# Key sums of the wide attention tiles from products with a constant column, in place of ScalarE's accumulator

## The chip, the cores and the metric

One core of a Trainium2 chip runs the whole program in one launch. The metric is the time of one execution on the device in microseconds (us), as the median of several runs. The profile is of one more execution of the same program.

## The reference

The program computes an attention stage and two feed-forward stages over 2304 tokens (4 batches of 576), in float32:

```python
a = softmax(scale * mean4(q) @ mean4(k)^T) @ mean4(v)      # 4 tokens averaged, every head
l = softmax(where(|i - j| < 4, scale * q @ k^T, -1e9)) @ v  # local band of 7 keys
x = repeat(a, 4) + l                                        # each softmax divides by its sum + 1e-9
xn = x / sqrt(mean(x*x) + 1e-6) * rms_g
h = (silu(xn @ w_gate) * (xn @ w_val)) @ w_out              # 512 -> 1536 -> 512
out = relu(h @ w_in)**2 @ w_out2                            # 512 -> 2048 -> 512
```

## The kernel before, in words

The feed-forward stages are float32 products, each made of three products of split operands (`xh`, `xl` are the high and low part of the activations, `whi`, `wlo` of the weights). The tokens are cut into nine blocks of 256. For block `j` and slice `fp` of the first hidden layer, `hidden` (L920) makes 24 gate products into bank `g` and 24 value products into bank `v`, and `outp` (L946) adds 24 products into banks `a` or `b`. One product of 256 columns is one instruction; there are 4080 of them, and 1632 of 512 columns in the second stage.

Before a block can be multiplied, its tokens must have gone through the attention stage. Batch 0 (blocks 0 and 1, and 64 tokens of block 2) goes through `wide` and `wide_post`: six tiles of 96 tokens (`WT`), each with a band of 104 keys (`WK`) and 8 heads. `wide(t)` (L702) makes the scores of the tile's 8 heads on TensorE, takes the maximum over the keys on VectorE, multiplies the maxima by the scale (L721), and runs one exponential per head on ScalarE (L725). Those 8 instructions per tile also give the sums over the keys through `accum_out`; L727 and L728 add 1e-9 to them and take the reciprocal, both on VectorE and in SBUF (`sums`, 96 x 8). Then the weights are transposed on TensorE and copied to `pt`. `wide_post(t)` (L737) multiplies `pt` with the values (L746, 8 products of 64 columns), spreads the averaged attention over the tokens (L751, 4 products of 128 columns), multiplies by the reciprocal of the sums, adds, squares and sums on ScalarE, takes the power on GpSimd, scales, transposes (L765) and writes `xh` and `xl` (L775, L776). The averaged attention itself comes from `down(b, pr)` (L614): per pair of heads three products of 144 columns, transposes, and 8 products of 65 columns. The other batches go through `attend` (a local attention on VectorE and GpSimd) and `post`.

The weights of the feed-forward stages are packed and are decoded on the chip: `decode` (L543) runs some seven instructions of 512 columns per half tile on ScalarE, VectorE and GpSimd. All of this preparation overlaps with the products as far as it can.

The order of the work is not the order of the source. Every operation is recorded with its dependences, and `Plan.trace` (L434) sets one order for all engines by planning: `PLAN` gives the order in which the steps are recorded (d: `down`, a: `wide`, b: `wide_post`, w: weights of a slice and kind, u: `attend`, p: `post`, x: `hidden` of one slice and `outp` of the one before), and the planner passes `ROUNDS` times over the operations, each time with first positions from the pass before, shifted at random by up to `JIT`, and keeps the best pass of its own reckoning. `TAGS` names the PSUM banks of each step, `SLOT` the buffers of the weights. On each engine instructions run in the order that comes out.

One more thing of the planner matters here. Until the first real product into the bank `v`, it fills planned idle time of TensorE with products of the identity with itself into that bank, which nobody reads:

```python
fill = fill and not op.ends
if fill and free:
    for _ in range(int((s - free) * FILL / 0.22)):
        self.nc.tensor.matmul(out=out, lhsT=one, rhs=one, start=True, stop=True)
```

They stand at L466 of the profile; all other instructions are issued by L473. `op.ends` (L333) is true of the first operation that writes bank `v` otherwise. From there on no fill product is made.

Of the kernel before, what the change touches and what calls it, by code (L numbers as in the profile page):

```python
# [17 lines left out]
AF = mybir.ActivationFunctionType  # L18
ALU = mybir.AluOpType
# [9 lines left out]
SCALE = 0.125  # L29
# [3 lines left out]
WT, WK = 96, 104  # L33
# [13 lines left out]


TAGS = ('dbg- dtg- dbg- dgg- bdd- bdd- bdd- bdd- ttd- ttd- ttd- ttd- add- add- add- add- '
        'aagg aagg aagt bbtd bbdd bbtd bdt tdt gta gdt gdt btt '  # L50
        '-- -- a3 a3 -- -- -- -- -- -- -- -- -- -- -- -- -- -- -- g1 g1 -- -- -- -- -- -- -- -- -- -- -- -- -- -- --')
SEQ = '011100001101'
PLAN = 'd2 d3 d0 d1 a0 b0 w00 a2 a1 w01 w12 b1 a4 b2 a3 a5 w11 w21 b4 w20 w10 b3 w02 w30 u1 w32 b5 d7 u0 d5 d4 d6 w22 E w31 w41 w40 w50 x x w42 x x d10 x x w52 w51 x x x x x p2 x u2 d11 u3 p3 x d8 x x u5 d9 u4 x x x p4 u6 x x d12 x x x d15 d14 d13 x u7 p5 u8 x u9 x x x x x p6 x x x u10 x x x u11 x x p7 x x u12 u13 x x x x x x x x p8 x x x x x x'
SLOT = [7, 8, 9, 1, 0, 4, 5, 2, 6, 3, 0, 1, 3, 4, 5, 2]
ROUNDS = 38
HIDE = 0.14
W2ST = 6
BEGIN = 1.6
# [1 line left out]
SPARE = {'A': 0.6, 'V': 2.2, 'P': -0.1}  # L60
SLACK = 0.02
FILL = 0.8
JIT = 0.3
SEED = 1


# [410 lines left out]
def attn_moe_kernel(ctx: ExitStack, tc, qs, kw, vw, qt, kt, vt, v4, wg, wv, wo, w2i, w2o, gw, gb,  # L477
                    msk, band, up, ones, ident, out):
    plan = Plan(tc.nc, tc, ctx)
    V, A, P, T, DQ, VP, AV = (plan.engine(e) for e in ("V", "A", "P", "T", "D", "VP", "AV"))  # L480

    start = [sum(BLK[:j]) for j in range(len(BLK) + 1)]
# [16 lines left out]
    def bank(tag, dtype=F32):  # L499
        return tile("ps", tag, [128, 512], dtype, 2 if tag in "ab" else 1)  # L500
# [8 lines left out]
    half_neg = tile("const", "half", [128, 8])  # L509
# [192 lines left out]
    def wide(t):  # L702

        v = wvs[t % len(wvs)]
        DQ.dma_start(out=v, in_=vt[WT * t:WT * t + WK])
        p, pt = wps[t % len(wps)], wpts[t % len(wpts)]
        bd = band_sb[:, 0 if t == 0 else 2 if t == S // WT - 1 else 1].unsqueeze(1).to_broadcast([WT, 4, WK])
        tags = TAGS.split()[16 + t]
        sp = [bank(tags[h])[0:WT, 0:4 * WK].rearrange("p (r k) -> p r k", r=4) for h in range(2)]
        with plan.joint():  # L710
            for h in range(2):
                T.matmul(out=sp[h], lhsT=id_sb[0:WT, 0:WT], rhs=bd, start=True, stop=False, skip_group_check=True)
            for r in range(4):
                for h in range(2):
                    hs = slice(64 * h, 64 * h + 64)
                    T.matmul(out=sp[h][:, r], lhsT=wq[r][hs, WT * t:WT * t + WT], rhs=wk[r][hs, WT * t:WT * t + WK],
                             start=False, stop=(r == 3), skip_group_check=True)
        nm, sm_ = small[t % 2][0], sums[t]
        for h in range(2):
            V.tensor_reduce(out=nm[:, 4 * h:4 * h + 4], in_=sp[h], axis=AX.X, op=ALU.max, negate=True)  # L720
        V.tensor_scalar(out=nm, in0=nm, scalar1=SCALE, scalar2=None, op0=ALU.mult)  # L721
        for h in range(2):
            for r in range(4):
                i = 4 * h + r
                A.activation(p[:, h, r], sp[h][:, r], AF.Exp, bias=nm[:, i:i + 1], scale=SCALE,  # L725
                             accum_out=sm_[:, i:i + 1])
        V.tensor_scalar(out=sm_, in0=sm_, scalar1=1e-9, scalar2=None, op0=ALU.add)  # L727
        V.reciprocal(out=sm_, in_=sm_)  # L728
        for h in range(2):
            tp = bank(tags[2 + h])[0:WK, 0:4 * WT].rearrange("p (r k) -> p r k", r=4)  # L730
            with plan.joint():
                for r in range(4):
                    T.transpose(tp[:, r], p[:, h, r], id_sb[0:WT, 0:WT])
            AV.copy(pt[:, h], tp)
        wx[t] = pt, v, sm_

    def wide_post(t):  # L737

        pt, v, rs = wx.pop(t)
        tags = TAGS.split()[22 + t]  # L740
        x = bank(tags[0])[0:WT]
        with plan.joint():
            for r in range(4):
                for h in range(2):
                    es = slice(128 * r + 64 * h, 128 * r + 64 * h + 64)
                    T.matmul(out=x[:, es], lhsT=pt[:, h, r], rhs=v[:, es], start=(r == 0 and h == 0),  # L746
                             stop=(r == 3), skip_group_check=True)
        y = bank(tags[1])[0:WT]
        with plan.joint():
            for r in range(4):  # L750
                T.matmul(out=y[:, 128 * r:128 * r + 128], lhsT=up_sb[:, t % 3], rhs=wod[r][:, t // 3],  # L751
                         start=(r == 0), stop=(r == 3), skip_group_check=True)
        xa, ss = wxas[t % 2], small[t % 2][1][:, 0:1]
        V.tensor_tensor(out=xa.rearrange("p (r h d) -> p r h d", r=4, h=2),
                        in0=x.rearrange("p (r h d) -> p r h d", r=4, h=2),
# [3 lines left out]
        V.tensor_scalar(out=ss, in0=ss, scalar1=1.0 / DM, scalar2=1e-6, op0=ALU.mult, op1=ALU.add)  # L759
        P.tensor_tensor(out=ss, in0=ss, in1=half_neg[0:WT, 0:1], op=ALU.pow)  # L760
        V.scalar_tensor_tensor(out=xa, in0=y, scalar=ss, in1=gb_sb, op0=ALU.mult, op1=ALU.mult)
        tp = bank(tags[2])[:, 0:4 * WT].rearrange("p (k n) -> p k n", k=4)
        with plan.joint():
            for k in range(4):
                T.transpose(tp[:, k], xa[:, 128 * k:128 * k + 128], id_sb[0:WT, 0:WT])  # L765
# [235 lines left out]
    s = 0  # L1001
    for c in PLAN.split():
        n = int(c[1:]) if c[1:] and c[0] != "w" else 0
# [175 lines left out]
```

## Time and profile before

| | before |
|---|---|
| median of 3 runs | 1000.95 us (1000.70 to 1002.62) |
| the profiled execution | 1000.25 us |
| its span, first to last instruction | 998.0 us |
| TensorE busy | 980.2 us, 98% of the span |
| VectorE busy | 587.6 us, 59% |
| ScalarE busy | 417.0 us, 42% |
| GpSimd busy | 442.3 us, 44% |

Times inside the profile count from the span's start. PE is TensorE, PEld its weight loads, DVE VectorE, ACT ScalarE, POOL GpSimd. Names of tiles stand without their numbers: `b` are the large buffers and also the PSUM banks of that letter, `w` the weight buffers, `st` the staging buffers of the decoding. A float32 product that is not split takes two passes, so 8 such products read as x16. PEclk is the share of TensorE's full clock that was granted.

### The profile page before, as it was taken

The numbers are of one execution on the slowest core, as the hardware profiler recorded it, in microseconds if no ns is written. First come the engines' busy times: TensorE is split into PE (matmuls) and PEld (weight loads), VectorE is DVE, ScalarE is ACT, GpSimd is POOL, SyncE is SP. The second block draws the span as 40 slices with busy tenths as digits, with TensorE's granted clock in tenths as the row PEclk, the third lists the DMA queues.
The fourth block names the chain that finished last, engine by engine and source line by source line (L and its number), as shares of the span: only waits on it lengthen the run. The fifth ranks groups of instructions, "written<-read, shape, count | busy, mean of one in ns | idle before, by whom it ended". The sixth has DMA issues, their size and how long they took to land.

```text
span 998.0 us, 17246 instructions
## 1 busy us (share of the span) xinstructions
PE 980.2 (98%) x6866; PEld 906.4 (91%) x6866; DVE 587.6 (59%) x985; ACT 417.0 (42%) x984; POOL 442.3 (44%) x298
## 2 busy tenths in 40 slices
PE   7998999999999999999999999999999999999998
PEld 7888999999999999999999998888888888888897
DVE  6999899786687857575634568963222322322232
ACT  5787665532435342323244557663222212322232
POOL 2566688867656676676733465863001000100000
PEclk9999999999999999999999999999999999999999
DMA  9954553253262523222011446334000100100010
GB/s 282 262 160 157 175 179 103 73 151 113 85 182 80 171 78 115 93 65 96 28 33 60 132 128 209 104 109 137 1 1 1 54 0 1 43 1 1 1 43 22
DMA packets 38465, 92.93 MB, mean 93 GB/s; under 512 B 4218, under 2 KB 14498, under 8 KB 38386
## 3 DMA queue, kind: packets, MB, share of 16 engines
q1 hardware_dynamic: 38386, 91.84, 29.6%
q8 instruction: 54, 0.88, 0.4%
q14 instruction: 25, 0.20, 0.1%
HBM read 80.62 MB, written 11.21 MB: 92 GB/s over the span
## 4 chain that ended last, share of the span: by engine, by line
PE 89%; DVE 5%; POOL 2%; DMA 2%; issue 1%; ACT 1%; SPq 0%; DVEq 0%; POOLq 0%; ACTq 0%
PE v L473 25%; PE g L473 24%; PE a L473 20%; PE b L473 15%; DVE b L473 2%; PE d L473 2%; DVE st L473 2%; PE t L473 2%; PE v L466 1%; DMA b<-in_qt 1%; DMA st<-in_wg 1%; POOL w L473 0%; POOL st L473 0%; POOL pr L473 0%; POOL b L473 0%
## 5 line engine op out<-in xcount | busy, mean ns | idle before, releaser
L473 PE MATMUL g<-xh,w 128*128 128x256 f32 (+1 forms) x776 | 176.8, 307 | 0.4 <-DVE th L473 0.4
L473 PE MATMUL v<-xh,w 128*128 128x256 f32 (+1 forms) x632 | 147.6, 311 | 0.5 <-DVE hl L473 0.5
L473 DVE SCALAR_TENSOR_TENSOR v<-v,th 128x512 f32<-128x512 f32 (+1 forms) x94 | 63.3, 674 | 128.6 <-ACT th L473 101.3
L473 PEld LDWEIGHTS g<-xh,w 128*128 128x128 f32 x776 | 131.1, 191 | 7.0 <-ACT xh L473 0.6
L473 ACT ACTIVATE th<-g 128x512 f32<-128x512 f32 (+1 forms) x94 | 54.5, 580 | 198.1 <-PE g L473 194.8
L473 POOL TENSOR_TENSOR pr<-v,es 128x896 f32<-128x896 f32 x54 | 99.4, 1939 | 65.7 <-DVE es L473 28.2
L473 PE MATMUL v<-xh,b 128*128 128x256 f32 (+1 forms) x552 | 123.9, 303 | 0.1
L473 POOL TENSOR_TENSOR pr<-k,q 128x896 f32<-128x896 f32 x54 | 115.4, 2158 | 9.6 <-DVE sc L473 7.2
L473 PE MATMUL g<-xl,w 128*128 128x256 f32 (+1 forms) x388 | 118.3, 305 | 0.1
L473 PEld LDWEIGHTS v<-xh,w 128*128 128x128 f32 x632 | 107.7, 191 | 7.1 <-PE g L473 0.7
L473 POOL TENSOR_TENSOR xl<-st,xh 128x1024 fp32r<-128x1024 f32 (+1 forms) x10 | 21.6, 2179 | 184.7 <-ACT xh L473 184.7
L473 PE MATMUL v<-xl,w 128*128 128x256 f32 (+1 forms) x316 | 97.9, 310 | 0.0
L473 PEld LDWEIGHTS v<-xh,b 128*128 128x128 f32 x552 | 93.0, 191 | 4.4 <-PE g L473 0.3
L473 PE MATMUL g<-xh,b 128*128 128x256 f32 (+1 forms) x408 | 94.4, 310 | 0.2 <-DVE th L473 0.2
L473 ACT CAST hh<-v 128x512 fp32r<-128x512 f32 (+1 forms) x94 | 53.5, 569 | 81.6 <-DVE v L473 71.3
L473 PE MATMUL v<-xl,b 128*128 128x256 f32 (+1 forms) x276 | 83.1, 301 | 0.0
L473 DVE SCALAR_TENSOR_TENSOR g<-g,th 128x512 f32<-128x512 f32 (+1 forms) x40 | 25.8, 645 | 95.5 <-ACT th L473 95.4
L473 DVE TENSOR_TENSOR hl<-v,hh 128x512 fp32r<-128x512 f32 (+1 forms) x94 | 62.4, 664 | 26.3 <-ACT hh L473 24.6
L473 PEld LDWEIGHTS g<-xl,w 128*128 128x128 f32 x388 | 74.1, 191 | 3.6 <-DVE xl L473 0.3
L473 POOL TENSOR_TENSOR st<-st 128x512 int32<-128x512 int32 x48 | 55.9, 1166 | 41.5 <-DVE st L473 39.4
L473 PEld LDWEIGHTS g<-xh,b 128*128 128x128 f32 x408 | 69.1, 190 | 4.2 <-issue 0.3
L473 ACT ACTIVATE st<-st 128x512 int32<-128x512 uint32 (+1 forms) x96 | 64.7, 684 | 18.7 <-DVE st L473 11.2
(207 smaller groups left out, 2336.8 us busy)
## 6 DMA issues: line engine op xcount, KB each, us to landing
k<-in_kw SPq DMA_DIRECT2D x12, 640.0 KB
v<-in_vw SPq DMA_DIRECT2D x12, 640.0 KB
st<-in_w2i SPq DMA_DIRECT2D x14, 512.0 KB
st<-in_w2o SPq DMA_DIRECT2D x14, 512.0 KB
y<-vv SPq DMA_DIRECT2D x18, 256.0 KB
out<-xh SPq DMA_DIRECT2D x18, 256.0 KB
st<-y SPq DMA_DIRECT2D x8, 512.0 KB
st<-in_wg SPq DMA_DIRECT2D x7, 512.0 KB
```

The source lines that it names most:

```text
L466: self.nc.tensor.matmul(out=out, lhsT=one, rhs=one, start=True, stop=True)
L473: getattr(self.hw[on[op]], method)(*args, **kw)
```

## The change

The sums over the keys no longer come from the exponentials. `wide` runs its 48 exponentials without `accum_out`. `wide_post` gets 8 products of one column per tile: the transposed weights `pt` (104 keys x 96 tokens) times a constant column of -0.5, into columns 384 to 391 of the bank that the transposes of the same tile use later. VectorE reads these sums from PSUM, multiplies by -2, adds 1e-9, and takes the reciprocal.

```diff
@@ wide
-                A.activation(p[:, h, r], sp[h][:, r], AF.Exp, bias=nm[:, i:i + 1], scale=SCALE,
-                             accum_out=sm_[:, i:i + 1])
-        V.tensor_scalar(out=sm_, in0=sm_, scalar1=1e-9, scalar2=None, op0=ALU.add)
-        V.reciprocal(out=sm_, in_=sm_)
+                A.activation(p[:, h, r], sp[h][:, r], AF.Exp, bias=nm[:, i:i + 1], scale=SCALE)
@@ wide_post, behind the products with the values
+        tp = bank(tags[2])
+        sm_ = tp[0:WT, 384:392]
+        with plan.joint():
+            for h in range(2):
+                for r in range(4):
+                    i = 4 * h + r
+                    T.matmul(out=sm_[:, i:i + 1], lhsT=pt[:, h, r], rhs=half_neg[0:WK, 0:1], start=(i == 0), stop=(i == 7),
+                             skip_group_check=True)
+        V.tensor_scalar(out=rs, in0=sm_, scalar1=-2.0, scalar2=1e-9, op0=ALU.mult, op1=ALU.add)
+        V.reciprocal(out=rs, in_=rs)
...
-        tp = bank(tags[2])[:, 0:4 * WT].rearrange("p (k n) -> p k n", k=4)
+        tp = tp[:, 0:4 * WT].rearrange("p (k n) -> p k n", k=4)
@@ numbers of the planner
-        'aagg aagg aagt bbtd bbdd bbtd bdt tdt gta gdt gdt btt '
+        'aagg aagg aagt bbtd bbdd bbtd bdt bdt gta gda gdt bdt '
...
-SLOT = [7, 8, 9, 1, 0, 4, 5, 2, 6, 3, 0, 1, 3, 4, 5, 2]
-ROUNDS = 38
+SLOT = [7, 8, 4, 1, 0, 9, 5, 2, 6, 3, 4, 1, 3, 2, 5, 0]
+ROUNDS = 14
...
-JIT = 0.3
+JIT = 0.05
```

`PLAN` is the same up to and with its first two steps x; behind them w42, w52, w51, d10, d8, u7, d13, u10, u12 and u13 stand one to some steps earlier or later among the steps x. With these numbers the planner gives another order from its start on. Two places matter below.

On TensorE, the first real product into bank `v` (`v<-xh`). Before, it stands behind 151 fill products, and behind all products with the values (96x64) of batch 0 and all but one of its groups of transposes to `xh` (128x96):

```order
L473 MATMUL b<-b_412,b_200 96x64 x8
L466 MATMUL v<-id 128x128 x19
L473 MATMUL t<-id,b_470 128x96 x4
L473 MATMUL d<-id,pe 72x96 x3
L466 MATMUL v<-id 128x128 x3
L473 MATMUL b<-b_351,qbd 96x144 x3
L473 MATMUL d<-id,pe 72x96 x3
L473 MATMUL t<-b_355,b_351 96x128
L473 MATMUL t<-b_410,b_351 96x128
L473 MATMUL t<-b_200,b_351 96x128
L473 MATMUL t<-b_294,b_351 96x128
L473 MATMUL v<-xh,w_796 128x256
```

In the change it stands behind 108 fill products, right behind the fifth of the six groups of sums (96x1):

```order
L466 MATMUL v<-id 128x128 x3
L473 MATMUL a<-half,b_358 96x1 x8
L466 MATMUL v<-id 128x128 x4
L473 MATMUL t<-id,b_502 104x96 x4
L466 MATMUL v<-id 128x128 x3
L473 MATMUL t<-half,b_402 96x1 x8
L473 MATMUL d<-id,b_502 104x96 x4
L473 MATMUL b<-b_354,qbd 96x144 x3
L473 MATMUL v<-xh,w_625 128x256
L473 MATMUL v<-xl,w_625 128x256
```

The rest of the wide tiles has moved behind the first 24 value products, between them and the first gate product, where no fill is made any more:

```order
L473 MATMUL t<-half,b_199 96x1 x8
L473 MATMUL a<-id,b_520 128x96 x4
L473 MATMUL d<-b_358,b_354 96x128
L473 MATMUL d<-b_402,b_354 96x128
L473 MATMUL d<-b_199,b_354 96x128
L473 MATMUL d<-b_298,b_354 96x128
L473 MATMUL b<-b_354,qbd 96x144 x3
L473 MATMUL g<-xh,w_450 128x256
```

On VectorE, the two instructions on the sums. Before, both work in SBUF (`b_89` to `b_89`), and the first of these rows is the scaling of the maxima, the second of that shape the addition to the sums:

```order
L473 TENSOR_SCALAR b_89<-b_89 96x8
L473 TENSOR_SCALAR st<-st 128x512
L473 TENSOR_SCALAR b_89<-b_89 96x8
L473 TENSOR_REDUCE xa<-pr 128x128
L473 TENSOR_SCALAR b_262<-b_262 128x512
L473 RECIPROCAL b_89<-b_89 96x8
```

In the change the addition reads the bank (`t`); the scaling of the maxima stays as it was:

```order
L473 TENSOR_SCALAR b_89<-b_89 96x8
L473 TENSOR_SCALAR st<-st 128x512
L473 TENSOR_SCALAR b_89<-t 96x8
L473 TENSOR_SCALAR ssum<-ssum 128x4
L473 RECIPROCAL b_89<-b_89 96x8
L473 TENSOR_SCALAR st<-st 128x512
```

## Rows read from the trace of the kernel before

**Rows 1.** The head of the page: span, busy time and share of each engine.

```profile
span 998.0 us, 17246 instructions
PE 980.2 (98%) x6866; PEld 906.4 (91%) x6866; DVE 587.6 (59%) x985; ACT 417.0 (42%) x984; POOL 442.3 (44%) x298
```

**Rows 2.** Busy time of each engine in stretches of the span.

```profile
core 0: us, PE busy (x) PEld busy (x) DVE busy (x) ACT busy (x) POOL busy (x), PEclk, DMA share, GB/s
50.00:75.00 25.00, 24.03 (x228) 21.65 (x227) 22.99 (x42) 20.74 (x61) 17.01 (x13) 1.00 0.51 160
75.00:100.00 25.00, 21.33 (x185) 20.79 (x184) 23.63 (x43) 19.13 (x47) 16.03 (x16) 0.93 0.48 156
200.00:250.00 50.00, 50.00 (x435) 50.00 (x434) 36.87 (x65) 17.23 (x50) 33.19 (x21) 1.00 0.45 132
```

**Rows 3.** PE in order of time, 30 to 106 us: start, length, instruction, wait before.

```profile
30.50 0.51 PE L473 MATMUL g<-id,b 96*104 96x96 f32 x4 [0.15 <-PE a L473]
...
79.69 1.08 PE L473 MATMUL d<-b,b 72*96 72x128 f32 x8 [1.63 <-DVE b L473]
...
95.32 0.47 PE L473 MATMUL v<-xh,w 128*128 128x256 f32 x1
...
99.47 0.90 PE L473 MATMUL b<-b,b 128*96 128x144 f32 x6
...
105.23 0.39 PE L473 MATMUL g<-xl,w 128*128 128x256 f32 x1
```

**Rows 4.** PE in order of time, products of 64 columns with the same weights as the sums.

```profile
32.75 1.50 PE L473 MATMUL b<-b,b 104*96 104x64 f32 x16
```

**Rows 5.** PE groups, 0 to 96 us: xcount | busy us, mean ns | idle before.

```profile
L466 PE MATMUL v<-id 128*128 128x128 f32 x302 | 40.9, 285 | 0.0
L473 PE MATMUL b<-w,w 64*96 64x104 f32 x48 | 2.9, 259 | 0.0
```

**Rows 6.** ACT in order of time: an exponential, its accumulator read, the next exponential.

```profile
34.06 0.33 ACT L473 ACTIVATE b<-a,b 96x104 f32<-96x104 f32 x1
34.29 0.20 ACT L473 ACTIVATION_READ_ACCUMULATOR b<-a,b 96x1 f32 x1
34.38 0.34 ACT L473 ACTIVATE b<-a,b 96x104 f32<-96x104 f32 x1
```

**Rows 7.** ACT groups, 0 to 100 us: reads of the accumulator, half of the wide tiles'.

```profile
L473 ACT ACTIVATION_READ_ACCUMULATOR b<-a,b 96x1 f32 x24 | 4.9, 203 | 0.0
```

**Rows 8.** DVE groups, 0 to 100 us: small instructions on SBUF and on PSUM.

```profile
L473 DVE TENSOR_SCALAR b<-b 96x8 f32<-96x8 f32 x12 | 5.2, 438 | 0.0
...
L473 DVE TENSOR_SCALAR b<-b 96x1 f32<-96x1 f32 x6 | 0.9, 142 | 0.0
...
L473 DVE TENSOR_SCALAR rc<-g 72x4 f32<-72x4 f32 x4 | 0.6, 150 | 1.7 <-PE g L473 1.7
```

**Rows 9.** DVE in order of time: the one held sum, and 78 to 105 us.

```profile
51.70 1.24 DVE L473 TENSOR_SCALAR b<-b 96x8 f32<-96x8 f32 x1
...
78.19 0.69 DVE L473 SCALAR_TENSOR_TENSOR b<-b 128x512 int32<-128x512 int32 x1
...
88.43 0.75 DVE L473 SCALAR_TENSOR_TENSOR b<-d,b,b 96x512 f32<-96x512 f32 x1 [1.32 <-POOL b L473]
89.10 2.10 DVE L473 SCALAR_TENSOR_TENSOR st<-st 128x512 int32<-128x512 int32 x1
...
92.98 1.41 DVE L473 TENSOR_SCALAR st<-st 128x512 f32<-128x512 f32 x1
...
102.03 0.98 DVE L473 SCALAR_TENSOR_TENSOR b<-b 128x512 int32<-128x512 int32 x1 [1.12 <-ACT b L473]
...
104.88 0.29 DVE L473 TENSOR_TENSOR xl<-t,xh 128x128 fp32r<-128x128 f32 x1 [0.29 <-ACT xr L473]
```

**Rows 10.** Stretches around the fall of TensorE's clock; columns as in rows 2.

```profile
88.60:92.00 3.40, 1.52 (x14) 1.39 (x15) 3.40 (x4) 1.25 (x3) 2.05 (x2) 1.00 0.97 317
92.00:95.40 3.40, 3.40 (x18) 3.34 (x18) 3.40 (x6) 2.54 (x6) 1.30 (x1) 0.52 0.45 172
```

More of the change, by code (lines that the diff above doesn't have):

```diff
@@ L49 @@
 TAGS = ('dbg- dtg- dbg- dgg- bdd- bdd- bdd- bdd- ttd- ttd- ttd- ttd- add- add- add- add- '
-        'aagg aagg aagt bbtd bbdd bbtd bdt tdt gta gdt gdt btt '
+        'aagg aagg aagt bbtd bbdd bbtd bdt bdt gta gda gdt bdt '
         '-- -- a3 a3 -- -- -- -- -- -- -- -- -- -- -- -- -- -- -- g1 g1 -- -- -- -- -- -- -- -- -- -- -- -- -- -- --')
 SEQ = '011100001101'
-PLAN = 'd2 d3 d0 d1 a0 b0 w00 a2 a1 w01 w12 b1 a4 b2 a3 a5 w11 w21 b4 w20 w10 b3 w02 w30 u1 w32 b5 d7 u0 d5 d4 d6 w22 E w31 w41 w40 w50 x x w42 x x d10 x x w52 w51 x x x x x p2 x u2 d11 u3 p3 x d8 x x u5 d9 u4 x x x p4 u6 x x d12 x x x d15 d14 d13 x u7 p5 u8 x u9 x x x x x p6 x x x u10 x x x u11 x x p7 x x u12 u13 x x x x x x x x p8 x x x x x x'
-SLOT = [7, 8, 9, 1, 0, 4, 5, 2, 6, 3, 0, 1, 3, 4, 5, 2]
-ROUNDS = 38
+PLAN = 'd2 d3 d0 d1 a0 b0 w00 a2 a1 w01 w12 b1 a4 b2 a3 a5 w11 w21 b4 w20 w10 b3 w02 w30 u1 w32 b5 d7 u0 d5 d4 d6 w22 E w31 w41 w40 w50 x x x w42 x d10 x x x x x w52 x w51 x p2 x u2 d11 u3 p3 x x d8 x u5 d9 u4 x x x p4 u6 x x d12 x x x d15 d14 u7 d13 x p5 u8 x u9 x x x x x p6 x x x x x x u10 u11 x x p7 x x x u13 x x x x x u12 x p8 x x x x x x x'
+SLOT = [7, 8, 4, 1, 0, 9, 5, 2, 6, 3, 4, 1, 3, 2, 5, 0]
+ROUNDS = 14
 HIDE = 0.14
```

## The prediction

> **What bounds the kernel now.** I read the head of the page first: TensorE is busy for 980.2 of 998.0 us [rows 1]. The stretches then tell where the rest lies: from 200 us on TensorE is busy for all of a stretch, at the full clock, while VectorE is busy for 36.87 of 50 us [rows 2]. After the start, then, the time is the number of products, and only a product more or less, or a gap, changes it. Between 50 and 100 us it is the other way round: TensorE stands between 21 and 24 of 25 us busy, but much of that is fill products, 302 passes with 40.9 us in all [rows 5], and VectorE is busy for 22.99 and 23.63 of 25 us [rows 2]. VectorE sets the pace there, with waits for GpSimd and ScalarE in between. So the question is when TensorE becomes full. I take for that point the first product of block 1 that needs the last `xl` of the wide tiles: in the kernel before it starts at 105.23 us [rows 3], just behind the VectorE instruction of 104.88 us that makes this `xl` [rows 9]. What TensorE has left to do at that point, added to the time of the point, is the span. (About 0.2%, 2 us, is what a measurement of this kernel can tell from no change.)
>
> **What the change removes.** An exponential of the wide tiles starts at 34.06, its accumulator read at 34.29, the next exponential at 34.38 [rows 6]. Without the read the next one could start at 34.29, so each of the 48 gives ScalarE back 0.09 us, 4.3 us in all, and at most the read's own length, 48 x 0.203 = 9.7 us [rows 7]. ScalarE is idle for 4.3 and 5.9 us in the two stretches of rows 2, so little of that is on the path. The row on it is the 1.12 us that VectorE waited for ScalarE at 102 us [rows 9]. I count half of this, 0.6 us, with 0 and 1.1 as bounds.
>
> **What it adds.** Six groups of 8 products of one column, each of two passes. The trace has no such product. Bounds: a 64-row product of 104 columns takes 2.9 us / 48 passes = 0.06 to 0.09 us with its weights [rows 5], and the 64-column products with the same weights take 1.50 / 8 = 0.19 us [rows 4]. I take 0.13, the middle, 1.04 us for a group, 6.2 us for all, 2.9 to 9.1 at the ends. All six groups stand ahead of block 1, where TensorE still has idle time or fill products, so they cost only as far as they move that time.
>
> VectorE's addition now reads PSUM. Five of the six additions before were short; one was held for 1.24 us instead of some 0.14 [rows 9], so 1.1 us is what can be saved there; the mean of 438 ns [rows 8] comes mostly from the scaling of the maxima, which stays. A read from PSUM costs no more by the rows: 150 ns for 72x4 from PSUM, 142 ns for 96x1 in SBUF [rows 8]. The Trainium skill says otherwise (Perfetto Trace Analysis, Optimizing Scalar/DVE Operations): an access of VectorE to PSUM has about 125 ns of overhead and one to SBUF about 60. By that the six additions would cost 0.4 us more; by the rows, which I follow, nothing.
>
> **What it moves.** The new order changes two things at once, and I price them in two steps.
>
> *Up to the first value product.* Compare the point of the kernel before at 79.69 us, the four products of 128 columns [rows 3], with the change's first value product. From the order, 123 fill products stand ahead of the first and 108 ahead of the second; one fill takes 40.9 / 151 = 0.27 us [rows 5], and the filled time is as long as the gap it fills, so 15 fewer are 4.1 us less. Of other products the change has ahead of its point: 40 of the sums more (5.2 us), 4 transposes of a wide tile more (0.3, as from 30.50 to 30.84 [rows 3]), 4 products of 128 columns fewer (0.9, rows 3 at 79.69), 8 products of 64 columns fewer (1.4, rows 4). 79.69 - 4.1 + 5.2 + 0.3 - 0.9 - 1.4 = 78.8 us. With the bounds of the sums it is 76.5 to 81. Before, that product came at 95.32 [rows 3]. The start is 16.5 us earlier, but it is not yet the point that counts.
>
> *From there to the last `xl` of block 1.* VectorE runs its list in order. In the change 43 instructions stand from the first value product to that `xl`; in the kernel before, the 43 instructions from 78.19 to 105.17 us [rows 9] do the same stretch of work. Priced with the usual length of each shape in the trace, the list before is 19.5 us and the new one 20.0 us. The old list took 27.0 us. The difference of 7.5 is waits (1.32 for GpSimd, 1.12 for ScalarE, 0.5 in small ones) and instructions that took longer than their like, as 2.10 us at 89.10 and 1.41 us at 92.98 [rows 9], while GpSimd was at work. The new list has as many instructions of the shapes that are held up, and GpSimd and ScalarE have as much to do beside it, so I let it lose the same, less the 0.6 us of ScalarE: 20.0 + 6.9 = 26.9 us. The `xl` is then made at 78.8 + 26.9 = 105.7 us, against 105.17: 0.5 us later.
>
> *What is left then.* As many products of the first stage are done at that point, 48. Of the rest, the change has three more transposes (0.25 us) and three more products of 144 columns (0.7 us, as the 0.90 us row at 99.47 less its tail [rows 3]) behind it. From some 100 products later on, both orders have the same work left. That is 1.0 us.
>
> *Later moves.* Weights, `down` and units of later blocks are recorded some steps earlier or later, and their DMAs with them. TensorE's queue of products covers that: it has no idle time between 200 and 250 us [rows 2]. In the new order the last `xl` of each later block stands at least 20 products ahead of its first use. If that cover failed, each block could cost one short gap. I count 0.
>
> **The sum:** 0.5 + 1.0 = 1.5 us over the profiled execution, whose 1000.25 us (span 998.0) lie 0.7 us under the median of the runs. On the median of 1000.95 that is **1002.5 us**, no difference that could be measured.
>
> **Rivals.**
>
> *TensorE's clock falls (slower).* In the kernel before, fill products stand almost up to the first value product; in 88.60 to 92.00 it was busy for only 1.52 of 3.40 us, and in the next 3.40 us the granted clock was 0.52, the 1.2 GHz level [rows 10]. In the change the fill ends at 78.8 us. Between the first value products and the first gate product TensorE has 4.2 us of work, VectorE 9.4 us by its list, some 13 us at its pace (x 27.0 / 19.5): TensorE idles for two thirds of the time. If the clock falls there, the work inside the gap still fits. The price falls due at its end: the 24 gate products of block 0 (2.9 us at full clock) stand ahead of the last transposes to `xh`, and the first products of block 1 follow. One half-clock stretch like that of rows 10 costs 1.7 us of full work; two of them make 3.4 us, 1002.5 + 3.4 = **1005.9 us**. It decides if the clock is low when the gate products start. The Trainium skill speaks for this one (TensorE: Matmul & The Clock Gate, Part 4: PE-mode transpose): transposes do not count as a busy TensorE in the way that products do, and part of the 4.2 us are transposes; no run here shows it by itself. Against it: a wait of 1.63 us, the one ahead of 79.69 [rows 3], did not lower the clock before.
>
> *VectorE's losses grow.* If more instructions meet GpSimd, as the one of 2.10 us did, two more such events are 2.7 us: 1005.2 us.
>
> *VectorE's losses vanish (faster).* If only the waits of 2.9 us remain and no instruction is held up, the list takes 22.9 instead of 26.9 us: 1002.5 - 4.0 = **998.5 us**. For it speaks that the adjoining stretches have instructions of the same shapes at their short lengths; against it, that GpSimd is busy for 16 of 25 us [rows 2] in all of this stage.
>
> *The change does not do what it says:* ScalarE's 4.3 us are real, but ScalarE waits there anyway; this is part of my forecast, not another time.
>
> **How the numbers follow.** No measurable difference 0.41, the clock 0.25, growing losses 0.12, vanishing losses 0.22. That gives faster 0.22, same 0.41, slower 0.37. The range reaches from the faster case, with 1 us for the bounds of the sums' price, to a little over the clock's case: 997.5 to 1007.
>
> **What would show it.** ScalarE's reads of the accumulator fall by 48 in the groups; the first value product starts near 78.8 us; the last `xl` of block 1 is made near 105.7 us; the groups of 96x1 products take some 1.0 us each; TensorE stays full from there on. The clock's case would show PEclk under 1.00 between 85 and 110 us and the gate products spaced twice as wide. I am wrong if the last `xl` comes more than 2 us from 105.7 us, or if TensorE has gaps behind it.

## The result, and the profile after

The changed kernel takes 1010.65 us (median of 4, 1008.43 to 1011.48) where the kernel before took 1001.49 beside it (median of 4): the ratio is 1.009, with an interval of 1.0072 to 1.0108. It is slower by some 9 us, beyond the end of the forecast's range (1007.0). The profiled execution took 1011.48 us, the longest of the four; its span is 1009.6, 11.6 us more than before.

The head of the page of the changed kernel answers to [rows 1]; the third line here is the clock granted to TensorE in 40 slices of the span:

```profile
span 1009.6 us, 17188 instructions
PE 988.9 (98%) x6876; PEld 914.1 (91%) x6876; DVE 594.8 (59%) x985; ACT 413.3 (41%) x936; POOL 443.4 (44%) x298
...
PEclk9979799999999999999999999999999999999999
```

ScalarE has 48 instructions less (936, 984 in [rows 1]): the reads are gone. The clock row is below 9 in the third and the fifth slice, 50 to 76 and 101 to 126 us with some 25 us a slice.

Busy time by stretches, with the columns of [rows 2]: first those three stretches, then four that follow the granted clock.

```profile
50.00:75.00 25.00, 24.51 (x175) 21.09 (x176) 17.77 (x39) 13.58 (x33) 10.30 (x8) 0.73 0.45 136
75.00:100.00 25.00, 22.91 (x212) 21.23 (x210) 22.44 (x36) 17.80 (x46) 21.71 (x17) 0.93 0.52 170
200.00:250.00 50.00, 50.00 (x421) 50.00 (x420) 38.23 (x66) 19.26 (x51) 38.23 (x24) 1.00 0.45 135
...
48.70:52.15 3.45, 1.66 (x17) 1.59 (x17) 3.45 (x6) 1.29 (x3) 1.43 (x2) 1.00 0.97 205
52.15:65.80 13.65, 13.65 (x74) 11.39 (x74) 7.82 (x19) 4.87 (x9) 4.51 (x3) 0.50 0.44 154
93.10:96.52 3.42, 2.09 (x18) 1.67 (x16) 3.42 (x2) 1.62 (x3) 3.31 (x3) 1.00 0.40 126
96.52:113.60 17.08, 12.53 (x61) 12.03 (x62) 15.59 (x30) 10.95 (x23) 7.59 (x8) 0.50 0.47 154
```

From 200 us on TensorE is busy for all of the stretch at the full clock, as in [rows 2]; the loss lies ahead of that. From 52.15 to 65.80 us TensorE is busy all the time, at 1.2 GHz, the lower level; from 96.52 to 113.60 it is at the lower level again. In the kernel before there was one such stretch in this part, of 3.41 us, in [rows 10]. And the roles have changed: between 50 and 75 us VectorE is busy for 17.77 us where it was busy for 22.99 [rows 2]. Here TensorE sets the pace and VectorE waits.

TensorE in order of time, as in [rows 3]:

```profile
50.49 0.54 PE L473 MATMUL t<-id,b 96*104 96x96 f32 x4 [2.53 <-DVE xl L473]
50.87 0.86 PE L466 MATMUL v<-id 128*128 128x128 f32 x6
51.60 2.27 PE L473 MATMUL t<-half,b 104*96 104x1 f32 x16
53.73 2.70 PE L473 MATMUL a<-half,b 104*96 104x1 f32 x16
56.29 2.80 PE L473 MATMUL g<-b,b 104*96 104x64 f32 x16
...
81.31 1.44 PE L473 MATMUL a<-half,b 104*96 104x1 f32 x16
82.61 1.14 PE L466 MATMUL v<-id 128*128 128x128 f32 x8
...
87.03 0.38 PE L473 MATMUL v<-xh,w 128*128 128x256 f32 x1
...
107.84 0.58 PE L473 MATMUL g<-xh,w 128*128 128x256 f32 x1 [0.74 <-DVE b L473]
...
116.24 0.39 PE L473 MATMUL g<-xl,w 128*128 128x256 f32 x1
```

TensorE stands for 2.53 us ahead of 50.49, waiting for an `xl`. Two groups of sums and a value group follow almost without fills. At full clock a group of sums takes 82.61 - 81.31 = 1.30 us, at the lower one 2.6 (53.73 to 56.29). The first value product comes at 87.03 us, forecast 78.8; the first product of block 1 that reads the last `xl` at 116.24, where it was 105.23 [rows 3].

VectorE in order of time, a usual conversion step of weights, three long ones, the late `xl`, and the last `xl` of block 1:

```profile
29.54 0.40 DVE L473 TENSOR_SCALAR b<-b 128x512 f32<-128x512 f32 x1
...
41.54 1.96 DVE L473 TENSOR_SCALAR st<-st 128x512 f32<-128x512 f32 x1
...
45.07 2.10 DVE L473 TENSOR_SCALAR st<-st 128x512 int32<-128x512 int32 x1
47.08 2.29 DVE L473 TENSOR_SCALAR b<-b 128x512 f32<-128x512 f32 x1
...
49.90 0.54 DVE L473 TENSOR_TENSOR xl<-t,xh 128x384 fp32r<-128x384 f32 x1
...
115.91 0.28 DVE L473 TENSOR_TENSOR xl<-t,xh 128x128 fp32r<-128x128 f32 x1
```

GpSimd beside the three long steps:

```profile
41.00 2.22 POOL L473 TENSOR_TENSOR pr<-v,es 128x896 f32<-128x896 f32 x1 [2.37 <-ACT b L473]
...
43.87 1.85 POOL L473 TENSOR_TENSOR pr<-v,es 128x896 f32<-128x896 f32 x1
45.59 1.29 POOL L473 TENSOR_TENSOR w<-st,w 128x512 fp32r<-128x512 f32 x1
46.94 2.16 POOL L473 TENSOR_TENSOR pr<-k,q 128x896 f32<-128x896 f32 x1
```

The three steps take 6.35 us in all, where three of 0.40 would take 1.2, and each ends within some 0.3 us of the end of a GpSimd instruction (43.50 beside 43.22, 47.17 beside 46.88, 49.37 beside 49.10). I call such a step held. The `xl` of 49.90, for which TensorE stands, is queued behind them.

### The profile page after: what moved, and what is told of

It is laid out like the page before. It is cut to its first block, busy times and chain, and to the rows that moved or that the text cites. A ratio compares the mean times of both kernels' runs of the same rounds, so it can differ in the third digit from the quotient of the medians.

```text
span 1009.6 us, 17188 instructions
## 1 busy us (share of the span) xinstructions
PE 988.9 (98%) x6876; PEld 914.1 (91%) x6876; DVE 594.8 (59%) x985; ACT 413.3 (41%) x936; POOL 443.4 (44%) x298
## 3 DMA queue, kind: packets, MB, share of 16 engines
q1 hardware_dynamic: 38386, 91.84, 29.3%
## 4 chain that ended last, share of the span: by engine, by line
PE 91%; DVE 4%; DMA 2%; issue 1%; ACT 1%; POOL 1%; SPq 0%; DVEq 0%; POOLq 0%; ACTq 0%
PE g L473 25%; PE v L473 24%; PE a L473 20%; PE b L473 16%; PE t L473 2%; PE v L466 2%; PE d L473 2%; DVE st L473 2%; DVE b L473 1%; DMA b<-in_wo 1%; DMA st<-in_w2i 1%; POOL w L473 1%; DMA id<-in_ident 0%; ACT st L473 0%; POOL b L473 0%
## 5 line engine op out<-in xcount | busy, mean ns | idle before, releaser
L473 PE MATMUL g<-xh,w 128*128 128x256 f32 (+1 forms) x776 | 179.3, 310 | 0.8 <-DVE b L473 0.7
L473 DVE TENSOR_SCALAR st<-st 128x512 f32<-128x512 f32 (+1 forms) x98 | 78.5, 803 | 8.6 <-ACT st L473 8.1
L473 POOL TENSOR_TENSOR st<-st 128x512 int32<-128x512 int32 x48 | 58.9, 1229 | 49.0 <-DVE st L473 44.2
```

What stands on the lines that cost most here:

```text
L473: getattr(self.hw[on[op]], method)(*args, **kw)
```

## The experiments

The theory after this reading: the held steps delay an `xl`, TensorE stands idle, its clock falls, and 13.65 us of filled time run at half clock; the second stretch follows from the early end of the fills. The first rival: the new sums themselves do it. The second: VectorE's list sets the end and the clock is a symptom. In all runs but order_alone and code_alone the order of the program is that of the change on every engine, except for what is shown. All ratios are to the kernel before on the same chip.

### The change once more, and its parts

**change_again**, without an edit.

> The changed kernel itself once more, on the chip of the next three runs. All theories expect 1008 to 1012 us. If the half-clock stretch at 52 us comes in nearly all executions, the mean granted clock is 0.984 to 0.988 in nearly all of them, as in the first four; if it were an accident of the profiled one, it would be 0.992 in most.

Ratio 1.0073 (1.0049 to 1.0097). The mean granted clock lies between 0.984 and 0.990 in all of its six executions; the profiled one has the same two stretches, 13.65 us from 51.01 and 10.24 us from 98.80. So it is no accident of one execution.

**order_alone**, the sums from ScalarE's accumulator, the numbers of the change (the tables of banks and of the plan too):

```diff
-SLOT = [7, 8, 9, 1, 0, 4, 5, 2, 6, 3, 0, 1, 3, 4, 5, 2]
-ROUNDS = 38
+SLOT = [7, 8, 4, 1, 0, 9, 5, 2, 6, 3, 4, 1, 3, 2, 5, 0]
+ROUNDS = 14
...
-JIT = 0.3
+JIT = 0.05
```

> The kernel before, with the table of banks, the order numbers and the planner's settings of the change; the sums still come from ScalarE's accumulator. If the loss comes with the products of the sums (theory: 8 products of one column cost 1.3 us of TensorE, and they stand in a stretch without fill products), the first value product comes near 80 us, the only half-clock stretch is a short one ahead of the gate products, and the time is 1000 to 1004 us. Rival: the loss comes with the new order (fills end earlier, VectorE's conversions of weights stand beside GpSimd's long products): 1007 to 1011 us with two half-clock stretches.

Ratio 1.0072 (1.0044 to 1.0100), 1008.98 us: the rival's outcome. Its first half-clock stretch is 6.83 us long, from 75.23. VectorE's row ahead of it, and GpSimd's beside that row:

```profile
69.94 6.37 DVE L473 TENSOR_SCALAR b<-b 128x512 f32<-128x512 f32 x1
...
69.39 2.10 POOL L473 TENSOR_TENSOR pr<-k,q 128x896 f32<-128x896 f32 x1
71.45 1.30 POOL L473 TENSOR_TENSOR w<-st,w 128x512 fp32r<-128x512 f32 x1
72.70 2.07 POOL L473 TENSOR_TENSOR pr<-k,q 128x896 f32<-128x896 f32 x1
74.73 1.29 POOL L473 TENSOR_TENSOR w<-st,w 128x512 fp32r<-128x512 f32 x1
```

One step of usually 0.4 us is held for 6.37 us, while GpSimd works without a pause from 69.39 to 76.02 us, and TensorE stands idle for the 4.53 us ahead of 77.02, waiting for VectorE.

**code_alone**, the products of the sums with the numbers of the kernel before, of which two entries in the table of banks are altered:

```diff
-        'aagg aagg aagt bbtd bbdd bbtd bdt tdt gta gdt gdt btt '
+        'aagg aagg aagt bbtd bbdd bbtd bdt bdt gta gdt gdt bdt '
```

> The products of the sums, with the order numbers and settings of the kernel before (in the table of banks one letter differs, so that no bank is asked for twice). Theory (most of the loss comes with the new numbers, as the run of the order alone had it at 1008.98 us; the products themselves cost TensorE 1.3 us a group): a time within 1001 to 1005 us and no long half-clock stretch ahead of 90 us. Rival (any order in which one-column products stand in a row without fills loses the clock): a half-clock stretch behind two groups of sums, and 1005 to 1011 us.

Ratio 1.0165 (1.0138 to 1.0191), 1019.47 us, worse than either, and above what theory and rival expected. Its stretches around the fall of the clock:

```profile
87.80:91.24 3.44, 0.47 (x5) 0.47 (x6) 3.08 (x6) 2.18 (x6) 3.29 (x3) 1.00 0.51 160
91.24:121.96 30.72, 20.76 (x101) 19.36 (x100) 28.48 (x50) 15.64 (x31) 22.14 (x18) 0.50 0.40 129
```

The first value product comes at 78.49 us here and ends the fills; TensorE is then busy for 0.47 of 3.44 us, and 30.72 us run at the lower clock. The loss therefore isn't the sum of two parts: each order has its own half-clock stretches, and the numbers of the change are the better ones for its code.

**reads_kept**, the accumulator reads put back into the change:

```diff
+                    if on[op] == "A" and kw.get("bias") is not None and args[0].parts == (0, WT) and args[0].index.shape == (WK,):
+                        kw = dict(kw, accum_out=spare[0:WT, 0:1])
```

> The change, with the accumulator reads of the 48 exponentials put back (their sums go to a spare column that nothing reads); products, order and results are as in the change. The forecast's step: 4.3 us of ScalarE's time, of which 0.6 us lies on the path: 0 to 1 us slower than the change, 1008 to 1012. Rival (the change gave nothing back there, since ScalarE waits anyway): no difference. Other rival (all of it was on the path): 1012 to 1015.

Ratio 1.0069 (1.0045 to 1.0094), no different from the change: what was taken off ScalarE gave nothing back that this run can tell.

### The first half-clock stretch

**more_fill_48us**:

```diff
-                        for _ in range(int((s - free) * FILL / 0.22)):
+                        n = int((s - free) * FILL / 0.22)
+                        runs += n > 0
+                        for _ in range(n + (12 if n and runs == 13 else 0)):
```

> The change, with 12 more fill products (24 passes, 2.6 us) just where TensorE stood idle for 2.53 us at 47.96 us; the order on every engine is else the same. Theory (the idle time makes the clock fall at 52.15 us, and the 13.65 us at half clock cost 6.8 us of TensorE's work): the stretch at half clock goes, the first value product comes near 81 us instead of 87.1, and the time falls by 4 to 7 us, to 1004 to 1007. Rival 1 (sums, transposes and 64-column products without fills do not hold the clock, whatever stood ahead): the clock falls one stretch later, at 55.6 us, and the time falls by less than 3 us. Rival 2 (VectorE's list sets the pace and the clock is a symptom): the stretch goes, but the last xl of block 1 still comes at 115 to 116 us, and the time stays within 2 us of 1010.65.

Ratio 1.0038 (1.0020 to 1.0056), 1005.33 us; 3.5 to 5 us better than the change, as the theory has it. The first value product comes at 83.46 us. But the stretches show that the theory is only half of it:

```profile
47.00:54.76 7.76, 7.76 (x80) 7.50 (x79) 7.65 (x13) 3.60 (x6) 4.47 (x4) 1.00 0.93 269
54.76:61.59 6.83, 6.83 (x35) 4.57 (x34) 4.06 (x11) 2.68 (x5) 2.48 (x2) 0.50 0.40 130
```

TensorE is busy for 7.76 of 7.76 us, and the clock falls all the same, only later and for half as long. In this time it did most of 36 passes of fills and 6 more, transposes, the two groups of sums and the first products of the value group.

**no_held_steps** and its control **no_free_steps** leave out three steps each, the held ones (7, 8, 9) or three of 0.4 us (2, 3, 4):

```diff
+                if on[op] == "V" and op.calls["V"][0][0] == "tensor_scalar" and size(op.calls["V"][0][2]["out"]) == 512:
+                    steps += 1
+                    if steps in (7, 8, 9):
+                        continue
```

> The change, without three of VectorE's conversion steps of weights (the TENSOR_SCALAR of 128x512 that start at 41.54, 45.07 and 47.08 us and took 1.96, 2.10 and 2.29 us, where their like takes 0.41): these steps are left out of the weights' decoding. Theory (these three were held by GpSimd's long products beside them; the xl of 49.90 us came late by that, TensorE stood idle for it, and the clock fell): the idle time of 2.53 us at 48 us goes, the clock does not fall at 52 us, and the time falls by 5 to 8 us. Rival (the clock falls for want of fills between 51.6 and 64 us, whenever the xl comes): the fall stays, somewhat earlier, and the time falls by no more than 3 us.

> The change, without three of VectorE's conversion steps of weights that were not held (the TENSOR_SCALAR of 128x512 at 29.54, 30.19 and 31.12 us, 0.40 to 0.42 us each): these steps are left out of the weights' decoding. The control to the run without the three held ones. Theory (being held is what costs: 6.35 us of the list in place of 1.2): the time stays within 2 us of the change's 1008 to 1011. Rival (VectorE's list sets the stage, and any three steps less free it): within 2 us of the 1004.62 of the run without the held ones.

Without the held steps the ratio is 1.0015 (0.9997 to 1.0032); without the three others it is 1.0074 (1.0055 to 1.0092), that of the change. VectorE in the control:

```profile
44.22 4.13 DVE L478 TENSOR_SCALAR st<-st 128x512 int32<-128x512 int32 x1
48.27 0.41 DVE L478 TENSOR_SCALAR b<-b 128x512 f32<-128x512 f32 x1
```

Of the second and third held step one now takes its 0.41 us and the other takes 4.13 instead: what is lost depends on GpSimd's work, not on which step meets it. So it is the holding that costs, some 6 us of time. In the run without the held steps TensorE had no idle time in the 6.40 us ahead of 52.90, and the clock fell again:

```profile
46.50:52.90 6.40, 6.40 (x70) 6.34 (x68) 5.79 (x9) 2.94 (x6) 5.20 (x4) 1.00 0.99 230
52.91:59.73 6.82, 6.82 (x34) 4.56 (x33) 4.42 (x10) 2.31 (x6) 3.44 (x3) 0.50 0.79 262
```

**sums_one_product** emits a group's 8 products as one of 8 columns:

```diff
+                if on[op] == "T" and "rhs" in calls[0][2] and calls[0][2]["rhs"].buf is self.half:
+                    kw = calls[0][2]
+                    calls = [("matmul", (), dict(kw, out=self.sums[op], rhs=self.eight, stop=True))]
```

> The change, with the 8 products of a sums group emitted as one product of 8 columns, whose weights are the first head's alone: the sums of the other 7 heads are left out. 42 products less, some 0.16 us each, 6.8 us of TensorE at full clock; the order is else the same. Theory (idle time at 48 us makes the clock fall): the fall at 52.15 us stays, the stretch at half clock gets shorter by the two groups inside it, and the time falls by 3 to 5 us. Rival (the sums themselves are the cause): the first half-clock stretch goes, the first value product comes near 79 us, and the time is 1000 to 1004 us.

Ratio 1.0011 (0.9996 to 1.0027), 1003.37 us, with no half-clock stretch ahead of 91.84 us in the profile: the rival's outcome. It takes 7 us of TensorE's work away as well as the products, so it can't tell the two apart. The next one can.

**sums_64_columns** keeps the number of products, the weights and the results:

```diff
+                    if op in self.sums and on[op] == "T":
+                        kw = dict(kw, out=self.sums[op][:, 64 * n:64 * n + 64], rhs=kw["rhs"].to_broadcast([WK, 64]))
+                    elif op in self.sums:
+                        kw = dict(kw, in0=self.sums[op].rearrange("p (i e) -> p e i", e=64)[:, 0])
```

> The change, with each product of the sums 64 columns wide in place of 1 (the constant column repeated); number of products, weights, order and results are the same. Theory 1 (the weights set the price of such a product, 0.163 us for one column against 0.166 for 64; and products of one column do not keep the clock, as the 64-column products do): a group still takes 1.3 us; the first half-clock stretch goes or is 6.8 us shorter, and the time falls by 3 to 7 us. Rival 1 (the idle time at 48 us alone makes the clock fall): the stretch from 52 us stays 13.65 us long and the time stays within 2 us of 1010.65. Rival 2 (columns set the price): a group takes over 2 us, and the time rises.

TensorE in its profile, a wait for an `xl`, a group of sums, what follows it, and the first value product:

```profile
49.70 0.54 PE L477 MATMUL t<-id,b 96*104 96x96 f32 x4 [0.67 <-DVE xl L477]
...
52.22 1.52 PE L477 MATMUL a<-half,b 104*96 104x64 f32 x16
53.58 1.52 PE L477 MATMUL g<-b,b 104*96 104x64 f32 x16
...
80.61 0.37 PE L477 MATMUL v<-xh,w 128*128 128x256 f32 x1
```

A group takes 1.36 us with 64 columns and 1.30 with one: 63 more columns are all but free. The ratio is 1.0047 (1.0029 to 1.0066). The profiled execution has no half-clock stretch ahead of 91.86 us, but it is the shortest of twelve, with a mean clock of 0.993; in eight of them the mean clock is 0.988 or less, as in the change. So width alone doesn't keep the stretch away in every execution. The twelve show what the clock is worth, as the program is the same: the four with a mean clock of 0.991 or more took 1003.2 to 1006.6 us, the eight others 1007.7 to 1012.3.

**wide_sums_more_fill**, this edit together with that of more_fill_48us:

> The 12 more fill products at 48 us, and the sums by products of 64 columns in place of 1, without fills between them; the order is else the same. Theory (columns, not the number of products, hold the clock): no half-clock stretch ahead of 90 us, mean granted clock 0.993, time 1001.5 to 1004 us, 2 us under the run with the 12 fills and one-column sums. Rival (width does not matter, only what stands between): the fall at 55 us stays, mean clock 0.991, time 1004.5 to 1006.5 us.

**held_and_wide**, this edit together with that of no_held_steps:

> The change, without the three held steps (left out of the weights' decoding), and with sums of 64 columns. Theory (the late xl and the one-column products are the whole of the first half-clock stretch): no half-clock stretch ahead of 90 us in nearly all executions, mean granted clock 0.992 to 0.996, first value product at 78 to 80 us, 1000 to 1002.5 us. Rival (something else makes the clock fall too): mean clock 0.991 or lower in half of them, 1003 to 1006 us.

The stretches of the two runs of one column above; in wide_sums_more_fill they lie 2.67 us later, as the products do:

```profile
49.67:57.43 7.76, 7.72 (x79) 7.47 (x79) 7.60 (x13) 3.61 (x6) 4.42 (x4) 1.00 0.95 264
57.43:64.26 6.83, 6.83 (x64) 5.72 (x63) 6.83 (x17) 4.00 (x11) 2.69 (x3) 1.00 0.44 142
```

and in held_and_wide:

```profile
46.50:52.90 6.40, 6.40 (x70) 6.34 (x69) 6.05 (x8) 3.12 (x6) 5.16 (x4) 1.00 0.98 271
52.90:59.73 6.83, 5.80 (x52) 4.50 (x50) 5.91 (x15) 3.03 (x6) 3.24 (x2) 1.00 0.67 229
```

Both times TensorE is busy in the first stretch as it was with one column, and the clock stays at 2.4 GHz. The mean clock is 0.991 to 0.996 over nine executions and 0.989 to 0.996 over twelve; what is missing in the profiled ones is the second stretch alone, 17.07 us and 13.65 us long. The ratios are 1.0023 (1.0001 to 1.0045) and 1.0018 (1.0001 to 1.0035).

In the profiles the four cases stand so: one column and 2.5 to 3.1 us of idle time, a stretch of 13.65 us (10.24 in reads_kept, with 1.85 us); one column without idle time, 6.83 us; 64 columns with 0.67 us of idle time, none in the profile and most executions with a low mean clock; 64 columns without idle time, none. One more profile belongs here, that of fill_after_value (below), whose sums have one column and whose 30 products stand later: 0.67 us of idle time, as in sums_64_columns, and again 13.65 us at the lower level.

```profile
47.12 0.54 PE L483 MATMUL t<-id,b 96*104 96x96 f32 x4 [0.67 <-DVE xl L483]
...
49.79:63.44 13.65, 13.65 (x71) 11.40 (x71) 9.84 (x24) 6.38 (x17) 4.97 (x4) 0.50 0.50 161
```

So the long idle time isn't needed for the long stretch, and the one-column products have more to do with it than the theory had. The first theory and the first rival are each half right; but each case is one profile, or a few, and executions of one kernel differ in their clock. The times don't follow, though: 1005.49 and 1003.57 us are 1 us or more above what the theory expected, and against no_held_steps the wide sums win nothing, where 2 us or more were expected.

**fill_between_sums**, the edit of more_fill_48us and 4 more fills behind each of three groups (two of sums, one of values; the lines of more_fill_48us are left out here):

```diff
+                    ahead = 4 if fill and free and runs == 14 else 0
+                        for _ in range(ahead):
+                            self.nc.tensor.matmul(out=out, lhsT=one, rhs=one, start=True, stop=True)
```

> The 12 more fill products at 48 us, as in the run that had them alone, and 4 more fill products behind each of the two groups of sums of 51.2 and 52.6 us and behind the value group after them (12, 2.6 us); the order is else the same. Theory (TensorE was busy without a gap from 44 to 54.76 us in the run with the first 12 alone, and the clock still fell for 6.83 us: the sums and what stands beside them do not hold it without fills between): the clock stays at full to 95 us, the mean granted clock is 0.993 or 0.994, and the time is as with the first 12 alone, 1003.5 to 1006, since 3.4 us of work are won and 2.6 us of fills paid. Rival (something further ahead makes it fall): the mean clock stays at 0.991 and the time rises by 2 us.

Ratio 1.0078 (1.0066 to 1.0090). In the profile the clock still falls, for 6.83 us from 55.00; the mean clock is anything from 0.987 to 0.996. It is inconclusive as to the clock; the time is 4 us worse than in more_fill_48us, also where the clock was high (1008.22 us at 0.996), and the first value product comes 2.9 us later (86.38), so TensorE's extra work is on the path here.

**fewer_fills**:

```diff
-FILL = 0.8
+FILL = 0.6
```

> The change with some 40 of its 123 fill products less (the share of a gap that is filled is 0.6 in place of 0.8); the order is else the same. Theory (fills keep the clock, and the stage is decided by it): the clock falls as early or earlier and for longer, and the time is 1010 to 1016 us. Rival (TensorE has too much to do ahead of the first value product, as VectorE's waits for it of 4.25 and 0.87 us show, and fills are a part of that): 9 us of TensorE's work less, the first value product comes 4 to 8 us earlier, and the time is 1003 to 1007 us.

Ratio 1.0058 (1.0039 to 1.0077), 1006.9 us. The time is the rival's, but the interval overlaps that of the change, and its mechanism isn't shown: in the profile, with 1010.30 us the longest of the six executions, the first value product comes at 87.96 us, no earlier than in the change, the stretch from 52.66 is again 13.65 us long, and a third one of 3.41 us appears at 86.79.

### The second half-clock stretch

**fill_after_value** adds 30 products of a zero tile behind the first value product, and **both_fills** has these and the 12 of more_fill_48us:

```diff
+                    if bank is not None and i <= gate:
+                        place += 1
+                        for _ in range({7: 8, 8: 18, 11: 4}.get(place, 0)):
+                            self.nc.tensor.matmul(out=bank.get()[:, 0:128], lhsT=zero, rhs=self.idle[1].get(),
+                                                  start=False, stop=False, skip_group_check=True)
```

> The change, with fill products that go on behind the first value product: 30 products of a zero tile, added into the running value bank (8 ahead of the sums group of 97.22 us, 18 behind it, 4 ahead of the first gate product); the order is else the same. Theory (the second stretch at half clock, 17.07 us from 96.52, comes from TensorE standing idle there, and costs what stands behind 107.8 us at half clock, some 6 us of time or 3 us of work): that stretch goes or ends before the gate products, and the time falls by 2 to 4 us, to 1006.5 to 1008.5. Rival (VectorE's list sets the time of the last xl, 115.91 us, whatever the clock): the stretch goes, the last xl stays at 115 to 116, and the time falls by less than 1.5 us.

> The 12 more fill products at 48 us and the 30 behind the first value product together. Theory (two independent half-clock stretches): the gains add up, 5.3 us of the first and 2 to 4 of the second, so 1001 to 1003.5 us. Rival (VectorE's list is what remains once the first stretch is shortened): no more than 1 us under the 1005.33 of the first alone.

Alone, 1.0050 (1.0035 to 1.0066): better than the change at its first measurement, but not clear of change_again. In the profile 3.41 us are left of the second stretch, as the theory of it has. With the 12 others 1.0037 (1.0018 to 1.0055), no better than the 12 alone (1.0038). In both_fills the clock stays high almost to the end of the stage:

```profile
63.63:111.40 47.77, 44.92 (x423) 41.39 (x421) 44.26 (x77) 35.12 (x88) 33.48 (x27) 1.00 0.46 143
```

But nothing is won by it. From the first value product to the end of the last `xl` of block 1 it takes 27.5 us in both_fills and 27.6 in fill_after_value, with 3.41 us at half clock, and 27.1 to 27.2 in more_fill_48us and change_again, with 10.24. In more_fill_48us the half clock lasted to 105.96 us, 3.3 us behind its first gate product, which is 1.6 us of work, and the `xl` came no later for it. Only where the second stretch is 17.07 us long (the change as first profiled, fill_between_sums, wide_sums_more_fill) does it take 29.2 to 29.3 us; with 13.65 it is 27.1 to 28.7.

## Why the prediction was wrong

**The bound, and the later blocks**: right. From 200 us on TensorE is full at the full clock, as in the kernel before, and the whole loss is there when the last `xl` of block 1 is made: 116.19 us against 105.17 is 11.0 of the 11.6 us of the span. The point was well chosen: in the kernel before and in all fourteen profiles with the order of the change, the span ends 892.0 to 893.4 us behind that `xl`.

**ScalarE's reads**: 0.6 us was counted; reads_kept finds nothing that can be measured, which fits the lower bound of 0, though 0.6 us is less than it could tell.

**The sums' price**: mis-sized, within its bounds. 0.13 us for a product was taken, the middle between two rows; 1.30 / 8 = 0.163 was measured, near the upper one. The lower row was misread: 2.9 us / 48 is the price of one pass [rows 5], and a product of the sums has two, so the lower bound was 0.12. And the middle had no reason: [rows 4], with the same weights, had the answer, since 64 columns cost hardly more than one (1.36 and 1.30 us a group). The Trainium skill has a price for the weights (TensorE: Matmul & The Clock Gate, LDWEIGHTS): a load takes a time in ns of the number of their columns / 1.2, by estimate 80 ns for 96 columns. The 0.163 us for two passes agrees; the products of [rows 5], with weights of 96 columns too, but on 64 rows, took 0.06 us a pass, which is less, and no run varied the weights. For five groups ahead of the point the difference is 1.3 us.

**VectorE's read from PSUM**: right. The groups of the changed kernel have it:

```profile
L473 DVE TENSOR_SCALAR b<-t 96x8 f32<-96x8 f32 x4 | 0.6, 161 | 2.4 <-PE t L473 2.4
L473 DVE TENSOR_SCALAR b<-a 96x8 f32<-96x8 f32 x2 | 0.3, 156 | 0.4 <-PE a L473 0.4
```

The six take 156 to 161 ns, as a step of this size in SBUF does where nothing holds it (0.16 us at 28.66 us). The extra cost that the Trainium skill's page (Perfetto Trace Analysis, Optimizing Scalar/DVE Operations) gives is not in the trace.

**Up to the first value product**: this is the step that failed, 78.8 us forecast, 87.0 measured. It said that "the filled time is as long as the gap it fills", so that all of it could be counted in fills at full clock. With the clock held the step was right: 80.61 us in the profile of sums_64_columns and 80.14 in held_and_wide, in the bounds of 76.5 to 81. What it left out is that the filled stretch itself could lose the clock. From 52.15 to 65.80 us the work of 6.8 us at full clock took 13.65. The 2.53 us of idle time don't come on top, since the kernel before stands idle too ahead of its point; this is TensorE's busy time from the start to the two points, first before, then in the change:

```profile
0.00:79.69 79.69, 70.43 (x653) 63.24 (x653) 68.37 (x135) 57.18 (x184) 39.13 (x37) 1.00 0.75 228
...
0.00:87.03 87.03, 78.58 (x682) 70.00 (x683) 70.39 (x133) 52.03 (x137) 40.50 (x37) 0.92 0.70 200
```

It is idle for 9.3 us before and for 8.5 in the change, 0.8 less. A fill takes 0.23 us at full clock (12 passes from 58.37 to 59.74 us in the kernel before), not the 0.27 of the forecast, whose mean holds slower ones at the start (18 passes from 7.00 to 10.55); 15 fewer save 3.4 us in place of 4.1, a loss of 0.6. With the 1.3 us of the sums the terms make 6.8 + 1.3 - 0.8 + 0.6 = 7.9 of the 8.2 us. In the fourteen profiles the first value product comes at 80.0 to 82.9 us where there is no first stretch, and at 81.8 to 88.0 where there is one. In sums_one_product, with some 6 us less of TensorE's work there, it comes at 80.02 us, against 80.61 in sums_64_columns: with the clock held, TensorE's work hardly sets the point, and the sums' 1.3 us may count only because the clock fell.

**From there to the last `xl`**: 26.9 us forecast; 29.2 in the changed kernel, 27.2 to 28.0 in change_again, both_fills, sums_64_columns and held_and_wide, 27.1 to 29.3 in all fourteen. The count of VectorE's list and its losses held; the 2 us more of the profiled execution go with its longer second half-clock stretch. So the second rival of the experiments is right that VectorE's last `xl` sets the end, but the clock is no mere symptom: the start of that list moves with it.

**What is left then**: 1.0 us forecast, 0.6 found.

**The rivals**: the clock's rival had the right mechanism and the second stretch, for which it gave 3.4 us; from the first gate product to 113.6 us half of 5.8 us is lost, 2.9. But it looked for the fall only where no fills stand, and the fall that costs most lies among them. The rival of VectorE's growing losses was priced at two events of 1.35 us; three held steps took 5.1 us more than usual, and, what it did not say, they lengthen the first half-clock stretch: without them it is 6.83 us long in place of 13.65. With the first stretch away the ratios are 1.0018 and 1.0023, where the forecast of 1002.5 us was 1.0015; as these runs leave steps out or add fills, that does not confirm the forecast. No version of the change was faster than the kernel before, not even with the sums almost free (1.0011).

## What to carry to other kernels

Price a product of one column from a row with the same weights and a few more columns: here 8 heads cost the same whether one column or 64 pass through their weights. When such products replace filler work, or a wait moves into the filled stretch, price the clock there too: the time a filled stretch takes is only known if it keeps its clock. And when a new order brings VectorE's steps over 128x512 beside a run of GpSimd's products, expect one of them to last until GpSimd pauses, as here, and look who is queued behind it.

## What the runs showed of the hardware

A busy TensorE can lose its clock: busy for 7.76 of 7.76 us and for 6.40 of 6.40 us, with 32 passes of one-column products among them, it fell to 1.2 GHz; with 64-column products of the same weights and nearly the same times it stayed at 2.4 GHz, both times. With 0.67 us of idle time ahead of the sums it fell with one column (fill_after_value) and stayed with 64 (sums_64_columns). These are single profiles, and other executions of sums_64_columns had a lower mean clock. What else stood there (transposes, the share of fills) was not taken apart.

A step of VectorE over 128x512 in SBUF, 0.40 us by itself, was held for 1.96 to 2.29 us, 4.13 us and, beside four GpSimd instructions in a row, 6.37 us. The Trainium skill (GPSIMD Engine Reference, Specifications) says that GpSimd shares its interfaces to SBUF with VectorE and that some of VectorE's modes contend with it; that one step can last through four of its instructions is what the trace adds. That it was the shared interface that held the step was not tested by itself.
